# Linear attention and two feed-forward layers on one core: loads one step earlier, stores one slot later, transposed sums in their own slot, and one unbroken run for the first layer's g

## The chip, the cores and the metric

The kernel runs on one core of one Trainium2 chip. The metric is device time in microseconds (us), the median of several executions. Beside it one execution was profiled, and every row below comes from that one.

## What is computed

Attention over 8 batches, 8 heads, 576 positions and head size 64, with a feature map of 128 columns used twice (once with each sign), followed by two feed-forward layers over 4608 tokens of width 512:

```python
def phi(x):
    proj = np.einsum('bhsd,df->bhsf', x, w_phi)
    proj = proj - np.max(np.abs(proj), axis=-1, keepdims=True)
    return np.concatenate([np.exp(proj), np.exp(-proj)], axis=-1)
...
kv = np.einsum('bhsf,bhsd->bhfd', k_p, v);  z = np.sum(k_p, axis=2)
num = np.einsum('bhsf,bhfd->bhsd', q_p, kv)
den = np.einsum('bhsf,bhf->bhs', q_p, z)[..., None] + 1e-06
x = num / den                       # then (tokens, heads * 64)
h = x @ w_in;  g = h - np.tanh(h);  x = g @ w_out          # first layer, 512 -> 2048 -> 512
out = ((x @ w1) * (x @ w2)) @ w3 @ w_out                   # second layer
```

## The kernel before

**Attention.** The program is written out by hand, and each engine runs its instructions in that order. Two batches with one head form a pair, so there are 32 pairs, and 33 steps, since a step holds the keys of one pair and the queries of the pair before it. A step has 9 tiles of 128 positions; four tiles make a slot, and slots do not line up with steps (9 slots cover 4 steps). In a slot `s` PE (TensorE) does, in this order: the projections of the slot's four tiles for q and k (`p_pe`, line 188), the transposes of the q tiles of slot s-1 (`t_pe`, 229), the products of keys and values of slot s-2 (`kv_pe`, 266), half an output of a pair where one is due (`o_pe`, 319 and 328), and, after the slot in which a pair's sums have been completed, two transposes and four small sums (`kv_turn`, 301 and 305). DVE (VectorE) takes maximum and difference of q and of k (`p_max`, 195 and 197), copies the finished sums out of the accumulator (`kvs`, 296), copies them again when they are transposed (`kvx`, 310), and copies every second output half (`st`, 340). PE's output needs `kvx`. ACT (ScalarE) does the exponentials, POOL (GpSimd) sums over keys. Pieces of the first layer's weights are turned from 64-bit floats into a high and a low 32-bit part in the gaps (`conv_steps`): `FC_EARLY` of 16 chunks per weight within the attention, the rest in the first layer.

In the kernel before the sums go through three slots: completed in one, copied (`kv_copy`) and transposed (`kv_turn`) in the next, copied again (`kv_out`) in the third, which is the slot where the output needs them. The SP queue issues all loads and stores: `qk` and `v` of step st+2 behind the last tile of step st, with two buffers for `qk` and three for `v`, and an output's stores right behind its copy.

**First layer.** 9 blocks of 512 tokens by 16 chunks of hidden features give 144 steps. In step n PE does `mm1(n)` (12 matmuls into `h`) and `mm2(n-2)` (12 matmuls of g's high and low part, `gh` and `gl`, into four accumulators `y`). Between the two stands `act_g`: ACT makes `u`, `t`, `s` (lines 480 to 482), DVE does five operations (486, 488, 490, 492, 494), ACT rounds the result to `gh` (498), POOL takes the rest as `gl` (499). Up to six operations of the weight conversions stand between DVE's five (`some()`), the others behind `gl`. At the end of a block the four `y` are copied out, three on ACT and one on DVE (513, 515). The second layer comes behind, and its code is not touched.

Of the kernel before, what the change touches and what calls it, by code (L numbers as in the profile page):

```python
# [45 lines left out]
TINY = 2.0 ** -15  # L46
FC_EARLY = 13


@with_exitstack  # L50
def kernel(ctx, tc, qk_in, v_in, w_phi, w_in, w_out, w12, w3t_in, wo2, out):
# [19 lines left out]
    slots = {}  # L71
    late = []

    def slot(kind, i, shape):
# [9 lines left out]
    def conv_steps(pool, pre, n, load, dst, nb=1):  # L84
# [7 lines left out]
        def s_abs():  # L92
            o["t"] = pool.tile([128, n], U32, tag=f"{pre}t", name=f"{pre}t", bufs=nb)
            ACT.activation(o["t"].bitcast(F32), words(o["raw"], F32)[1], ACTF.Abs)
# [23 lines left out]
        def s_lo():  # L118
            POOL.tensor_tensor(o["lo"], o["t"].bitcast(F32), o["hi"].bitcast(F32), ALU.subtract)

        return [s_load], [s_abs, s_max, s_shift], [s_c, s_a], [s_add], [s_hi], [s_lo]

# [26 lines left out]
    def attention():  # L149
        with ExitStack() as es:  # L150
# [19 lines left out]
            def load_step(st):  # L170
                qk[st] = pool.tile([128, PT], F32, tag="qk", name="qk")
                SP.dma_start(qk[st], qk_in[st])
                if st < NPAIR:
                    vv[st] = pool.tile([128, TPP + 1, D], F32, tag="v", name="v", bufs=3)
                    SP.dma_start(vv[st], v_in[st])
# [160 lines left out]
            def o_out(st, c, ps):  # L336
                bp, h = divmod(st - 1, H)
                t = pool.tile([128, CW + CE], F32, tag="st", name="st")
                if c:
                    DVE.tensor_copy(t, ps[:, :CW + CE])  # L340
                else:
                    ACT.activation(t, ps[:, :CW + CE], ACTF.Copy)
                for b in range(2):
                    c0 = bp * PT + b * S + c * CW
                    SP.dma_start(num_d[h * D:(h + 1) * D, c0:c0 + CW], t[b * D:(b + 1) * D, :CW])
                    for e in range(2):
                        r = 64 * b + 32 * e
                        SP.dma_start(den_d[bp, h:h + 1, c0 - bp * PT + e * CE:c0 - bp * PT + (e + 1) * CE], t[r:r + 1, CW:])
                return bp if c and h == H - 1 else None
# [36 lines left out]
            ok = lambda g: 0 <= g < n_slots  # L386
            kv_done, turned, todo_o = None, None, []
            for s in range(n_end):
# [7 lines left out]
                if ok(s):  # L396
                    p_pe(s)
                if kv_done is not None:
                    kv_copy(kv_done)
                if ok(s - 1):  # L400
# [3 lines left out]
                if ok(s):  # L404
                    dq[s] = p_max(s, pq, q_js(s), "q")
                for st, c, ps in todo_o:
                    bp = o_out(st, c, ps)
                    if bp == NBP - 1:
                        pending.extend([lambda: recip_load(NBP - 1), lambda: recip(NBP - 1)])
                    elif bp is not None:  # L410
                        recip_load(bp)
                        extra[s + 4].append(lambda bp=bp: recip(bp))
                if turned is not None:
                    kv_out(turned)
                some(2)
                turned = kv_done
                if ok(s - 1):
                    q_exp(s - 1, 0)
                    q_exp(s - 1, 1)
                    kv_sum(s - 1)  # L420
                kv_done = kv_pe(s - 2) if ok(s - 2) else None
                if ok(s):
                    dk[s] = p_max(s, pk, k_js(s), "k")
                todo_o = [(st, c, o_pe(st, c)) for st, c in o_at.get(s, [])]
                if turned is not None:
                    kv_turn(turned)
                some(99)
                for n in tiles_of(s) if ok(s) else ():
                    st, t = where(n)
                    if t == TPP - 1 and st + 2 < n_steps:  # L430
                        load_step(st + 2)
# [29 lines left out]
    def moe1():  # L461
        with ExitStack() as es:
# [6 lines left out]

            def act_g(n, x, ys):  # L470
                def some():
                    if x:
                        x.pop(0)()
# [15 lines left out]
                some()  # L489
                DVE.scalar_tensor_tensor(p, s, C0, p, ALU.add, ALU.mult)  # L490
                some()
                DVE.tensor_scalar(u, u, TLIM * TLIM, None, ALU.is_le)  # L492
                some()
                DVE.copy_predicated(t, u.bitcast(U32), p)  # L494
                some()
# [4 lines left out]
                y_out(ys, 3)  # L500
                del hh[n]
                gg[n] = gh, gl
# [15 lines left out]
            def mm2(n):  # L518
# [4 lines left out]
                gh, gl = gg.pop(n)  # L523
                for d in range(NK):
                    c = slice(d * 128, (d + 1) * 128)
                    for m, (w, x) in enumerate(((wh, gh), (wl, gh), (wh, gl))):
                        PE.matmul(  # L527
                            yy[j][d], w[:, c], x, start=i == 0 and m == 0, stop=i == NFC - 1 and m == 2
                        )
                return (j, yy.pop(j)) if i == NFC - 1 else None  # L530
# [49 lines left out]
            for n in range(n_all + LAG):  # L580
# [17 lines left out]
                if n < n_all:  # L598
                    x = list(extra.get(n, []))
                    act_g(n, x, ys)  # L600
                    for f in x:
                        f()
                    if i % 3 == 0 and i < 12:
# [201 lines left out]
```

## Time and profile before

| | |
|---|---|
| median of 3 runs | 1864.66 us (1863.5 to 1865.66) |
| profiled execution | 1864.26 us, of which the profile's span is 1862.5 us |
| PE, matmuls | busy 1797.4 us, 97% of the span |
| DVE, ACT, POOL | busy 53%, 42%, 40% |
| DMA | 168.86 MB, 91 GB/s over the span |

A share is an average over the whole span; attention, first and second layer differ much. A busy PE is not a PE at full rate: a matmul's recorded time overlaps that of the next one, so the distance from one start to the next tells the rate.

### The profile page before, as it was taken

How to read it: one execution, taken by the hardware profiler on the slowest of the kernel's cores; microseconds unless marked ns; L12 is line 12 of the kernel's file. 1: busy time of each engine (PE TensorE's matmuls, PEld its weight loads, DVE VectorE, ACT ScalarE, POOL GpSimd, SP SyncE). 2: the span in 40 equal slices, each digit the busy share in tenths (PEclk: the TensorE clock that was granted, in tenths of full speed). 3: DMA queues.
4: the chain of work that ended last, by engine and by line, in shares of the span. 5: the costliest groups of instructions: out<-in, count | busy, mean ns of one | idle time of the engine just before them, and what ended most of it. 6: DMA issues, size and time to landing. Idle time of an engine off the chain costs nothing.

```text
span 1862.5 us, 27570 instructions
## 1 busy us (share of the span) xinstructions
PE 1797.4 (97%) x10176; PEld 1409.6 (76%) x10176; DVE 995.1 (53%) x1649; ACT 785.0 (42%) x1601; POOL 744.3 (40%) x750
## 2 busy tenths in 40 slices
PE   7999899999999999999999999999999999999999
PEld 5666666667777777777777777878888888888887
DVE  6777777847677777777777776521121112112111
ACT  4656566535555555545555555422122112112211
POOL 5767677725455655555555564300011001001100
PEclk9999999999999999999999999999999999999999
DMA  4444445422233333333333324552001101100100
GB/s 151 143 144 153 148 152 175 122 65 64 65 94 96 99 101 108 100 97 100 99 98 102 114 91 148 174 175 84 30 23 40 34 29 29 41 34 23 35 23 23
DMA packets 99944, 168.86 MB, mean 91 GB/s; under 512 B 13920, under 2 KB 46048, under 8 KB 99808
## 3 DMA queue, kind: packets, MB, share of 16 engines
q1 hardware_dynamic: 99648, 167.02, 28.6%
q8 instruction: 80, 1.31, 0.3%
q14 instruction: 56, 0.46, 0.1%
q10 hardware_dynamic: 160, 0.07, 0.0%
HBM read 117.46 MB, written 49.58 MB: 90 GB/s over the span
## 4 chain that ended last, share of the span: by engine, by line
PE 52%; DVE 22%; ACT 16%; issue 5%; DMA 3%; SPq 1%; ACTq 0%; DVEq 0%; POOL 0%
PE ab L456 21%; PE o L657 11%; DVE p L490 6%; DVE t L494 6%; ACT gh L498 4%; DVE u L492 4%; PE y L527 3%; ACT u L480 3%; PE p L188 3%; PE h L456 3%; ACT s L482 3%; PE o L319 3%; PE o L680 2%; PE kv L266 2%; DVE et L104 2%
## 5 line engine op out<-in xcount | busy, mean ns | idle before, releaser
L499 POOL TENSOR_TENSOR gl<-t,gh 128x512 fp32r<-128x512 f32 x144 | 186.6, 1296 | 287.6 <-ACT gh L498 202.9
L748 POOL TENSOR_TENSOR xl<-xn,xh 128x512 fp32r<-128x512 f32 x72 | 93.6, 1299 | 498.7 <-ACT xh L747 498.6
L498 ACT ACTIVATE gh<-t 128x512 fp32r<-128x512 f32 x144 | 91.0, 632 | 367.0 <-DVE t L494 338.9
L527 PE MATMUL y<-gl,woh 128*128 128x512 f32 x576 | 231.4, 402 | 13.9 <-POOL gl L499 12.8
L527 PE MATMUL y<-gh,woh 128*128 128x512 f32 x576 | 228.2, 396 | 14.6 <-DVE yo L515 7.1
L486 DVE SCALAR_TENSOR_TENSOR p<-h,u 128x512 f32<-128x512 f32 x144 | 99.6, 692 | 234.5 <-ACT t L481 234.5
L527 PE MATMUL y<-gh,wol 128*128 128x512 f32 x576 | 224.8, 390 | 0.0
L456 PE MATMUL h<-xh,wih 128*128 128x512 f32 x576 | 224.3, 389 | 0.0
L456 PE MATMUL h<-xh,wil 128*128 128x512 f32 x576 | 224.1, 389 | 0.0
L456 PE MATMUL h<-xl,wih 128*128 128x512 f32 x576 | 224.1, 389 | 0.0
L456 PE MATMUL ab<-xh,wih 128*128 128x512 f32 x576 | 224.1, 389 | 0.0
L456 PE MATMUL ab<-xh,wil 128*128 128x512 f32 x576 | 224.1, 389 | 0.0
L456 PE MATMUL ab<-xl,wih 128*128 128x512 f32 x576 | 224.1, 389 | 0.0
L639 DVE TENSOR_TENSOR t<-ab,a 128x512 f32<-128x512 f32 x72 | 49.8, 692 | 297.4 <-PE ab L456 294.4
L527 PEld LDWEIGHTS y<-gl,woh 128*128 128x128 f32 x576 | 108.0, 188 | 60.1 <-POOL gl L499 38.6
L527 PEld LDWEIGHTS y<-gh,woh 128*128 128x128 f32 x576 | 108.2, 188 | 45.1 <-DVE yo L515 10.1
L195 DVE TENSOR_REDUCE m<-p 128x4 f32<-128x512 f32 (+1 forms) x145 | 98.7, 681 | 80.4 <-PE p L188 80.0
L494 DVE COPY_PREDICATED t<-u,p 128x512 f32<-128x512 uint32 x144 | 127.4, 885 | 3.2
L208 ACT ACTIVATE kp<-dk 128x512 f32<-128x512 f32 x144 | 82.9, 626 | 109.6 <-DVE dk L197 75.3
L490 DVE SCALAR_TENSOR_TENSOR p<-s,p 128x512 f32<-128x512 f32 x144 | 128.2, 890 | 0.0
L456 PEld LDWEIGHTS h<-xh,wih 128*128 128x128 f32 x576 | 108.1, 188 | 22.8 <-issue 0.2
L456 PEld LDWEIGHTS h<-xh,wil 128*128 128x128 f32 x576 | 108.2, 188 | 22.6
(106 smaller groups left out, 3539.7 us busy)
## 6 DMA issues: line engine op xcount, KB each, us to landing
qk<-in_qk SPq DMA_DIRECT2D x33, 576.0 KB
v<-in_v SPq DMA_DIRECT2D x32, 320.0 KB
xn<-y_d SPq DMA_DIRECT2D x37, 256.0 KB
num_d<-st SPq DMA_DIRECT2D x128, 72.0 KB
xn<-num_d SPq DMA_DIRECT2D x36, 256.0 KB
out<-o SPq DMA_DIRECT2D x36, 256.0 KB
y_d<-yo SPq DMA_DIRECT2D x35, 256.0 KB
eraw<-in_w SPq DMA_DIRECT2D x32, 256.0 KB
```

Of the source, the lines that this page charges most:

```text
L195: DVE.tensor_reduce(m[:, :n], what[g][:, j], AX.X, ALU.max, apply_absolute_value=True)
L208: ACT.activation(kp[g][:, sgn, span(js)], dk[g][:, span(js)], ACTF.Exp, scale=1.0 - 2 * sgn)
L456: PE.matmul(ps, a[:, kk, :], b[kk], start=m == 0, stop=m == 3 * NK - 1)
L486: DVE.scalar_tensor_tensor(p, h, C2, u, ALU.mult, ALU.mult)
L490: DVE.scalar_tensor_tensor(p, s, C0, p, ALU.add, ALU.mult)
L492: DVE.tensor_scalar(u, u, TLIM * TLIM, None, ALU.is_le)
L494: DVE.copy_predicated(t, u.bitcast(U32), p)
L498: ACT.activation(gh, t, ACTF.Copy)
L499: POOL.tensor_tensor(gl, t, gh.bitcast(F32), ALU.subtract)
L527: PE.matmul(yy[j][d], w[:, c], x, start=i == 0 and m == 0, stop=i == NFC - 1 and m == 2)
L657: PE.matmul(ps, a[:, c], w, start=m == 0, stop=m == 23)
L748: POOL.tensor_tensor(lo, a, hi.bitcast(F32), ALU.subtract)
```

## The change

`qk` gets three buffers and `v` four, and both are loaded behind the first tile of step st, not the last. The output's stores are listed in the next slot, and the four small stores of the denominators become one. A pair's sums are copied and transposed in the slot that completes them, and copied again at the start of the next slot. `FC_EARLY` falls from 13 to 12 (the buffers take its room), so the first layer converts 16 half chunks and not 12; their stages are split in one more step and 14 steps hold their starts. In the first layer DVE's five operations stand together; ACT's conversions stand before `gh`, DVE's and POOL's behind `gl`. The copy of the fourth `y` moves up to DVE's third place. In `mm2`, except for the first and last chunk of a block, the four matmuls on `gl` come last. The buffers of the converted word `et` go from 3 to 4; the raw words `eraw` keep 2.

```diff
-FC_EARLY = 13
+FC_EARLY = 12
...
-                qk[st] = pool.tile([128, PT], F32, tag="qk", name="qk")
+                qk[st] = pool.tile([128, PT], F32, tag="qk", name="qk", bufs=3)
...
-                    vv[st] = pool.tile([128, TPP + 1, D], F32, tag="v", name="v", bufs=3)
+                    vv[st] = pool.tile([128, TPP + 1, D], F32, tag="v", name="v", bufs=4)
...
                 if ok(s):
                     p_pe(s)
+                for x_ in todo_store:
+                    bp = o_store(*x_)
...
                 if kv_done is not None:
-                    kv_copy(kv_done)
+                    kv_out(kv_done)
+                todo_store = [o_out(*x_) for x_ in todo_o]
...
-                if turned is not None:
-                    kv_out(turned)
-                some(2)
-                turned = kv_done
...
                 kv_done = kv_pe(s - 2) if ok(s - 2) else None
+                some(2)
+                if kv_done is not None:
+                    kv_copy(kv_done)
                 if ok(s):
                     dk[s] = p_max(s, pk, k_js(s), "k")
                 todo_o = [(st, c, o_pe(st, c)) for st, c in o_at.get(s, [])]
-                if turned is not None:
-                    kv_turn(turned)
+                if kv_done is not None:
+                    kv_turn(kv_done)
                 some(99)
...
-                    if t == TPP - 1 and st + 2 < n_steps:
+                    if t == 0 and st + 2 < n_steps:
                         load_step(st + 2)
...
                 DVE.scalar_tensor_tensor(p, h, C2, u, ALU.mult, ALU.mult)
-                some()
                 DVE.tensor_tensor(t, h, t, ALU.subtract)
-                some()
+                y_out(ys, 3)
                 DVE.scalar_tensor_tensor(p, s, C0, p, ALU.add, ALU.mult)
...
+                for f in x:
+                    if f in on_act:
+                        f()
                 gh = p3.tile([128, 512], F32R, tag="gh", name="gh")
...
+                todo = [(d, m) for d in range(NK) for m in range(3)]
+                if 0 < i < NFC - 1:
+
+                    todo.sort(key=lambda a: a[1] == 2)
...
-            for i in range(FC_EARLY, NFC):
-                for f in (w_in_chunk, w_out_chunk):
+            for f in (w_in_chunk, w_out_chunk):
+                for i in range(FC_EARLY, NFC):
                     for part in range(2):
                         c = f(p2, i, part, 2, "e", 3)
-                        late_chunks.append([c[0], c[1], c[2] + c[3] + c[4] + c[5]])
+                        late_chunks.append([c[0], c[1], c[2] + c[3], c[4] + c[5]])

             for i, c in enumerate(late_chunks):
-                place(c, i)
+                place(c, i * 14 // len(late_chunks))
```

DVE early in the attention, from one slot's maximum of q to the next slot's. `m` and `dq`, `dk` are maxima and differences, `ct` a weight conversion, `st` an output half. Before:

```order
L195 TENSOR_REDUCE m<-p 128x4
L197 TENSOR_TENSOR dq<-p,m 128x512
L340 COPY st<-o 128x432
L310 COPY kvx<-kv 128x260
L104 SCALAR_TENSOR_TENSOR ct<-craw,ct 128x512
L195 TENSOR_REDUCE m<-p 128x4
L197 TENSOR_TENSOR dk<-p,m 128x512
L296 COPY kvs<-kv 128x256
L195 TENSOR_REDUCE m<-p 128x4
```

And now, in the same slot:

```order
L342 COPY st<-o 128x432
L197 TENSOR_REDUCE m<-p 128x4
L199 TENSOR_TENSOR dq<-p,m 128x512
L105 SCALAR_TENSOR_TENSOR ct<-craw,ct 128x512
L298 COPY kvs<-kv 128x256
L197 TENSOR_REDUCE m<-p 128x4
L199 TENSOR_TENSOR dk<-p,m 128x512
L312 COPY kvx<-kv 128x260
L197 TENSOR_REDUCE m<-p 128x4
```

`kvs` has moved ahead of the slot's k, and `kvx` to the head of the next slot, ahead of its q; the copy `st` has moved to the head of its slot.

DVE in the first layer, step 30, from the first of g's operations to the last conversion (`et` is a piece of the second layer's weights). Before:

```order
L486 SCALAR_TENSOR_TENSOR p<-h,u 128x512
L488 TENSOR_TENSOR t<-h,t 128x512
L104 SCALAR_TENSOR_TENSOR et<-eraw,et 128x256
L490 SCALAR_TENSOR_TENSOR p<-s,p 128x512
L492 TENSOR_SCALAR u<-u 128x512
L494 COPY_PREDICATED t<-u,p 128x512
L98 TENSOR_SCALAR et<-et 128x256
L101 TENSOR_SCALAR et<-et 128x256
```

And now:

```order
L489 SCALAR_TENSOR_TENSOR p<-h,u 128x512
L490 TENSOR_TENSOR t<-h,t 128x512
L492 SCALAR_TENSOR_TENSOR p<-s,p 128x512
L493 TENSOR_SCALAR u<-u 128x512
L494 COPY_PREDICATED t<-u,p 128x512
L105 SCALAR_TENSOR_TENSOR et<-eraw,et 128x256
L99 TENSOR_SCALAR et<-et 128x256
L102 TENSOR_SCALAR et<-et 128x256
```

All conversions of the step now stand behind g's five operations.

ACT in step 2 of the first layer, where half chunks are converted (`et<-eraw` takes up a raw piece for the first time, `ec<-eraw` reads an older one again). Before:

```order
L480 ACTIVATE u<-h 128x512
L481 ACTIVATE t<-h 128x512
L482 ACTIVATE s<-u,c_sb 128x512
L109 ACTIVATE ec<-eraw 128x256
L116 ACTIVATE wih_5238<-et 128x256
L94 ACTIVATE et<-eraw 128x256
L498 ACTIVATE gh<-t 128x512
```

And now:

```order
L484 ACTIVATE u<-h 128x512
L485 ACTIVATE t<-h 128x512
L486 ACTIVATE s<-u,c_sb 128x512
L110 ACTIVATE ec<-eraw 128x256 x2
L95 ACTIVATE et<-eraw 128x256
L502 ACTIVATE gh<-t 128x512
```

Two pieces are under way instead of one. The third piece, which `et<-eraw` takes up here, is loaded into a raw buffer that the first piece frees with its last DVE operation (line 105 of the changed kernel), and that operation now stands behind g's five of this same step.

## Rows read from the trace of the kernel before

**Rows 1.** Busy time by stretch: attention, first layer, second layer (us, instruction counts)

```profile
41.10:389.00 347.90, 326.63 (x3689) 223.25 (x3689) 259.88 (x430) 203.16 (x442) 242.77 (x288) 1.00 0.46 142
389.00:1231.50 842.50, 814.04 (x3484) 645.98 (x3480) 591.17 (x1007) 441.68 (x915) 436.40 (x396) 1.00 0.33 103
1231.50:1862.00 630.50, 626.20 (x2760) 518.03 (x2760) 118.36 (x171) 120.83 (x202) 41.46 (x32) 1.00 0.13 42
```

**Rows 2.** Timeline, two slots: start, duration, engine, line [idle before, releaser]

```profile
321.04 1.08 PE L266 MATMUL kv<-kp,v 128*64 128x256 f32 x8
...
322.40 0.42 DVE L310 COPY kvx<-kv 128x260 f32<-128x260 f32 x1
...
322.87 1.19 PE L319 MATMUL o<-qp,kvx 128*64 128x288 f32 x8 [0.75 <-DVE kvx L310]
...
326.29 1.08 PE L266 MATMUL kv<-kp,v 128*64 128x256 f32 x8
...
327.21 1.14 PE L319 MATMUL o<-qp,kvx 128*64 128x288 f32 x8
```

**Rows 3.** Waits within 41 to 389 us: sum, times, longest

```profile
PE o L319 <- DVE kvx L310: 9.6, 17, 1.3
...
PE kv L266 <- DVE kvx L310: 6.4, 6, 2.2
...
PE p L188 <- DMA qk<-in_qk: 2.7, 3, 1.4
```

**Rows 4.** Timeline, a projection whose load was late

```profile
158.03 0.72 PE L188 MATMUL p<-wphi,qk 64*128 64x128 f32 x8 [1.15 <-DMA qk<-in_qk]
```

**Rows 5.** Stretches at the start, columns as in rows 1, PE's clock third last

```profile
25.00:27.00 2.00, 0.42 (x6) 0.36 (x4) 1.97 (x4) 2.00 (x6) 2.00 (x4) 1.00 0.06 25
27.00:35.00 8.00, 8.00 (x49) 5.58 (x47) 6.35 (x11) 3.90 (x8) 6.59 (x8) 0.57 0.32 97
```

**Rows 6.** Timeline of the first layer's first step, conversions and POOL absent

```profile
395.32 0.69 DVE L486 SCALAR_TENSOR_TENSOR p<-h,u 128x512 f32<-128x512 f32 x1 [5.59 <-ACT t L481]
...
397.58 0.72 DVE L494 COPY_PREDICATED t<-u,p 128x512 f32<-128x512 uint32 x1
...
398.34 0.63 ACT L498 ACTIVATE gh<-t 128x512 fp32r<-128x512 f32 x1 [2.51 <-DVE t L494]
...
399.98 0.69 DVE L486 SCALAR_TENSOR_TENSOR p<-h,u 128x512 f32<-128x512 f32 x1 [1.67 <-ACT t L481]
```

**Rows 7.** Groups of the first layer, 389 to 1231 us: count, busy, mean ns

```profile
L499 POOL TENSOR_TENSOR gl<-t,gh 128x512 fp32r<-128x512 f32 x144 | 186.6, 1296 | 287.6 <-ACT gh L498 202.9 <-issue 49.0 <-DMA xr<-rden_d 24.3
L490 DVE SCALAR_TENSOR_TENSOR p<-s,p 128x512 f32<-128x512 f32 x144 | 128.2, 890 | 0.0
L494 DVE COPY_PREDICATED t<-u,p 128x512 f32<-128x512 uint32 x144 | 127.4, 885 | 3.2
...
L492 DVE TENSOR_SCALAR u<-u 128x512 f32<-128x512 f32 x144 | 87.2, 605 | 0.0
...
L104 DVE SCALAR_TENSOR_TENSOR et<-eraw,et 128x256 uint32<-128x256 uint32 x92 | 47.6, 517 | 0.0
...
L747 ACT ACTIVATE xh<-xn 128x512 fp32r<-128x512 f32 x36 | 22.2, 616 | 0.0
```

**Rows 8.** Waits of the first layer, 389 to 1231 us

```profile
DVE p L486 <- ACT t L481: 234.5, 144, 5.6
...
PE y L527 <- POOL gl L499: 12.8, 25, 0.7
...
PE y L527 <- DVE yo L515: 7.1, 7, 1.3
...
ACT u L480 <- PE h L456: 4.2, 8, 0.6
```

**Rows 9.** A raw piece's load and the DMA after it (last two columns: share, GB/s)

```profile
407.38 0.34 SPq L145 DMA_DIRECT2D eraw<-in_w_out  x1
...
410.00:411.00 1.00, 1.00 (x6) 0.65 (x4) 0.75 (x3) 0.61 (x2) 0.00 (x0) 1.00 0.00 0
```

More of the change, by code (lines that the diff above doesn't have):

```diff
@@ L72 @@
     late = []
+    on_act = set()
     def slot(kind, i, shape):
@@ L92, in s_abs @@
         def s_abs():
-            o["t"] = pool.tile([128, n], U32, tag=f"{pre}t", name=f"{pre}t", bufs=nb)
+            o["t"] = pool.tile([128, n], U32, tag=f"{pre}t", name=f"{pre}t", bufs=nb + (nb > 1))
             ACT.activation(o["t"].bitcast(F32), words(o["raw"], F32)[1], ACTF.Abs)
@@ L119, in s_lo @@
             POOL.tensor_tensor(o["lo"], o["t"].bitcast(F32), o["hi"].bitcast(F32), ALU.subtract)
+        on_act.update((s_abs, s_c, s_hi))
         return [s_load], [s_abs, s_max, s_shift], [s_c, s_a], [s_add], [s_hi], [s_lo]
@@ L337, in o_out @@
                 bp, h = divmod(st - 1, H)
-                t = pool.tile([128, CW + CE], F32, tag="st", name="st")
+                t = pool.tile([128, CW + CE], F32, tag="st", name="st", bufs=3)
                 if c:
@@ L342, in o_out, with o_store @@
                     ACT.activation(t, ps[:, :CW + CE], ACTF.Copy)
+                return t, bp, h, c
+            def o_store(t, bp, h, c):
                 for b in range(2):
@@ L345, in o_out @@
                     SP.dma_start(num_d[h * D:(h + 1) * D, c0:c0 + CW], t[b * D:(b + 1) * D, :CW])
-                    for e in range(2):
-                        r = 64 * b + 32 * e
-                        SP.dma_start(den_d[bp, h:h + 1, c0 - bp * PT + e * CE:c0 - bp * PT + (e + 1) * CE], t[r:r + 1, CW:])
+                d = den_d[bp, h, c * CW:]
+                SP.dma_start(
+                    bass.AP(tensor=d.tensor, offset=d.offset, ap=[[S, 2], [CE, 2], [1, CE]]),
+                    t.rearrange("(a p) n -> a p n", p=32)[:, 0, CW:],
+                )
                 return bp if c and h == H - 1 else None
@@ L386, in attention @@
             ok = lambda g: 0 <= g < n_slots
-            kv_done, turned, todo_o = None, None, []
+            kv_done, todo_o, todo_store = None, [], []
             for s in range(n_end):
@@ L397, in attention @@
                     p_pe(s)
+                for x_ in todo_store:
+                    bp = o_store(*x_)
+                    if bp == NBP - 1:
+                        pending.extend([lambda: recip_load(NBP - 1), lambda: recip(NBP - 1)])
+                    elif bp is not None:
+                        recip_load(bp)
+                        extra[s + 4].append(lambda bp=bp: recip(bp))
                 if kv_done is not None:
-                    kv_copy(kv_done)
+                    kv_out(kv_done)
+                todo_store = [o_out(*x_) for x_ in todo_o]
                 if ok(s - 1):
@@ L405, in attention @@
                     dq[s] = p_max(s, pq, q_js(s), "q")
[L406 to L412, printed above, removed]
-                if turned is not None:
-                    kv_out(turned)
-                some(2)
-                turned = kv_done
                 if ok(s - 1):
@@ L468, in moe1, with act_g @@
             gg, yy = {}, {}
[L470 to L473, printed above, removed]
+            def act_g(n, ys):
                 h = hh[n]
@@ L484, in act_g @@
                     y_out(ys, d)
-                some()
                 DVE.scalar_tensor_tensor(p, h, C2, u, ALU.mult, ALU.mult)
-                some()
                 DVE.tensor_tensor(t, h, t, ALU.subtract)
-                some()
+                y_out(ys, 3)
                 DVE.scalar_tensor_tensor(p, s, C0, p, ALU.add, ALU.mult)
-                some()
                 DVE.tensor_scalar(u, u, TLIM * TLIM, None, ALU.is_le)
-                some()
                 DVE.copy_predicated(t, u.bitcast(U32), p)
-                some()
+                x = extra.get(n, [])
+                for f in x:
+                    if f in on_act:
+                        f()
                 gh = p3.tile([128, 512], F32R, tag="gh", name="gh")
@@ L499, in act_g @@
                 POOL.tensor_tensor(gl, t, gh.bitcast(F32), ALU.subtract)
-                y_out(ys, 3)
                 del hh[n]
@@ L523, in mm2 @@
                 gh, gl = gg.pop(n)
[L524 to L529, printed above, removed]
+                todo = [(d, m) for d in range(NK) for m in range(3)]
+                if 0 < i < NFC - 1:
+                    todo.sort(key=lambda a: a[1] == 2)
+                for d, m in todo:
+                    w, x = ((wh, gh), (wl, gh), (wh, gl))[m]
+                    PE.matmul(
+                        yy[j][d], w[:, d * 128:(d + 1) * 128], x,
+                        start=i == 0 and m == 0, stop=i == NFC - 1 and m == 2,
+                    )
                 return (j, yy.pop(j)) if i == NFC - 1 else None
@@ L598, in moe1 @@
                 if n < n_all:
[L599 to L602, printed above, removed]
+                    act_g(n, ys)
+                    for f in extra.get(n, []):
+                        if f not in on_act:
+                            f()
                     if i % 3 == 0 and i < 12:
```

## The prediction

> **What bounds the kernel now.** I read the busy time by stretch first, because the shares over the whole span hide which engine waits. In the second layer PE has 2760 matmuls in 626.2 busy us, one every 0.2269 us, without a pause worth naming. The first layer has the same kind of matmul, 144 steps of 24 and 24 more from the second layer's first two halves, 3480 in all; at that rate they need 789.6 us, and the stretch lasts 842.5 us. So 52.9 us are lost there, though PE reads busy in 814 of 842.5 us [rows 1]. In the attention PE is the busiest too (326.6 of 347.9 us), DVE next with 259.9 (75%).
>
> Then the timeline, for what a lost moment looks like. In a slot without a wait the output starts 0.92 us behind the key-value products (326.29 to 327.21); in the slot before it 1.83 us, waiting for `kvx`, which ended at 322.82 [rows 2]. The recorded wait is 0.75, the loss 0.91: a stop costs 0.16 us beyond its recorded length.
>
> Then the table of waits. In the attention PE waits for `kvx` 9.6 and 6.4 us, 23 times, and 2.7 us, 3 times, for `qk` [rows 3]. In the first layer it waits for `gl` (25 times) and for the copies of `y` [rows 8]; and behind that, DVE's first operation of every step waits for ACT's `t`, 234.5 us in 144 steps, while ACT's `u` almost never waits for PE's `h` (8 times, 4.2 us). The pace of that layer is thus set by a loop of DVE and ACT: five operations, `gh`, `u`, `t`, and round again; PE stands behind it. All matmuls are at the full clock but for a short stretch at the start [rows 1, 5].
>
> **The change part by part.** The sum is made against the profiled execution's 1864.26 us, which is 0.4 us under the median; a difference of 0.2% (3.7 us) is about what a measurement of this kernel can tell from none.
>
> *Sums a slot earlier (gain 19.7).* `kvx` now runs at the head of the slot after the one that completes the sums, and the output needs it one slot later still. The 23 waits go: 16.0 us recorded and 23 times 0.16 beyond, 19.7 us [rows 2, 3]. The new wait is PE's transposes for `kvs` in the same slot; between them and the key-value products stands an output half, at least 1.19 us of PE work, and the copy takes DVE some 0.42 (as `kvx`) [rows 2], so it is covered unless DVE is over 0.8 us late. Behind `kvs` on DVE stands the slot's k, for which the next slot's projections wait. In the first few slots no output half is due, and there I count neither gain nor loss.
>
> *Loads a step earlier (gain 3.2).* The wait of 1.15 us at 158.03 and two like it go [rows 3, 4]: 2.7 us and three times 0.16. The merged stores take issues off SP; SP has no other wait on PE's path, so this counts nothing, as does the later listing of the stores, for which a third `st` buffer is there.
>
> *What DVE takes back (loss 5).* Without PE's pauses DVE has 259.9 us of work in some 325 us, 80%, but not evenly: every nine slots two short ones follow each other (one with no sums to transpose, then one without an output), and DVE has as much to do in them as in others: two maxima, two differences, a copy, often a conversion. The trace has no row for this; bounds are 0 (DVE catches up, as it does in most such places now) and 10 (over 1 us in each of 8 rounds, as much as the wait it replaces). I take 5. Attention: 19.7 + 3.2 - 5 = 18.
>
> *First layer, the loop.* In the first step, with POOL idle, the five operations take from 395.32 to 398.30, and from there to the next first operation it is 1.68 us: a loop of 4.66 us [rows 6]. In the mean over all steps the last three are longer by 0.21, 0.19 and 0.165 (890, 605 and 885 ns against 0.68, 0.42 and 0.72 in that step), in all 0.57. Every fourth step on average ACT also splits an `x` in between, 36 times 0.616 us, 0.15 a step [rows 7]. So the bare loop is 5.38 us, PE's step 24 times 0.2269, 5.45. What made the loop longer are DVE's conversions between the five; behind them they fall into the 1.68 us in which DVE waits for ACT anyway (the largest, `et`, takes 0.52 [rows 7]; all three of a piece, by that row an estimate of 1.2, and 0.64 pieces a step). If that cover were gone they would cost up to 0.8 us a step. The loop falls just under PE's step, and PE becomes the bound. With `gl` last in 14 of 16 chunks POOL has 6 matmuls, 1.36 us, more time; and the fourth `y` is copied before DVE's third operation, so the waits for `y` go too. Of the 52.9 us I keep: 0.7 for the first `gl`, which is still wanted third; an estimated 6 for the unevenness of a loop that is only 1% under PE's step (bounds 0 and 13, a quarter of today's loss); and the next item.
>
> *Late half chunks (loss 6).* In steps 2, 8 and 9 ACT takes up a raw piece whose buffer is freed only in the same step, by the conversion behind g's five operations, and `gh` stands behind it. From the end of the five it is 0.52 for `et`, then the load: issued at 407.38, its data were in before 410.00, so at most 2.6 us [rows 7, 9]; with ACT's 0.4 some 3.5 us in which `gh`, the next `u` and all behind them stand. `gh` is otherwise 2.8 us ahead (12 matmuls three times are 8.2 us, the way from `h` to `gh` about 5.4). One such step alone costs 3.5 less some 1.8 of lead at the start, two in a row 7.0 less 2.8: together 6. Bounds: 0, if the copy of the load comes sooner than it shows, and 10 without any lead. The lower `FC_EARLY` moves two chunks' work from one layer to the other and counts nothing beyond this.
>
> First layer: 52.9 - 0.7 - 6 - 6 = 40. **Sum:** 1864.3 - 18 - 40 = 1806.
>
> **Where a rule would have it otherwise.** The last three of g's operations [rows 6, 7] are 0.57 us a step above the undisturbed ones, no more, though POOL works in about half of that time. The Trainium skill, "SBUF — State Buffer", section "Who interferes with whom", says that VectorE and GpSimd share a pair of ports under an exclusive lock, and whichever comes second stands still until the first is done. By this rule a run of DVE's three operations beside `gl` could lose a whole `gl` in each step; by the trace it does so in part.
>
> **The rivals.**
> 1. *The loop stays the bound.* If the gathered run meets POOL more often and loses 0.8 instead of 0.57, the loop is 5.61; 144 of them and 13 us of start and tail are 821, with 6 for the late chunks 827: the layer gains 15 only. 1864.3 - 18 - 15 = 1831. For it: only 1% between the loop and PE's step. Against it: POOL's conversions now come after `gl`, so more of them fall on DVE's conversions and on the 1.68 us without work, not on the last three operations.
> 2. *The attention's gain is spent elsewhere.* PE stops for `dq` where it stopped for `kvx`, and only 5 of 22.9 us stay: 1819. For it: DVE at 80%. Against it: 80% still leaves DVE 65 us, and `dq` is made ahead of what the slot adds.
> 3. *Slower.* The gathered run waits out a whole `gl` (1.30 us) in every step: loop 6.1, layer 13 + 880 + 6 = 899, 57 more than now: 1903. From 1.03 us a step on (loop 5.84, layer 860) the attention's 18 are eaten up and the kernel is slower. Against it: the mean of 0.57, which already holds many meetings.
> 4. *All of it.* DVE takes nothing back, only 2 us stay in the first layer, and the half clock near 28 us, which followed a stretch with PE busy 0.42 of 2 us [rows 5], does not come (8 us at a mean of 0.57 cost 3.4): 1864.3 - 22.9 - 50.9 - 3.4 = 1787.
>
> **Chances.** Forecast 0.58, with a range of its own from 1797 to 1817; rival 1 0.14, rival 2 0.13, rival 3 0.05, rival 4 0.06, and 0.04 for what I have not seen. From 1789 to 1833 lie the forecast, rivals 1 and 2. Faster by over 0.2%: 0.94; within 0.2%: 0.02; slower: 0.04, since rival 3 mostly ends beyond its deciding point.
>
> **What would show it.** Attention: no wait of the output for `kvx`; from key-value products to output 0.92 us in each slot; waits of projections for `dq` show what was given back. First layer: a block of 16 steps in 87 to 88 us where it is some 92.5 now (842.5 less the ends, over nine), DVE's wait for `t` much shorter, `u` now waiting for `h` often, and three waits of ACT for `eraw` near the layer's beginning, each with a stop of PE. The prediction is wrong if `u` still hardly ever waits for `h`: then the loop is still the bound.

## The result and the profile after

The changed kernel takes 1875.73 us (median of 4 runs, 1873.54 to 1877.36) beside 1864.91 for the kernel before: ratio 1.0058, 95% interval 1.0041 to 1.0076. It is 0.6% slower, where 1806 was forecast. The profiled execution is 1876.69 us, its span 1874.9.

Busy time by stretch of the changed kernel, columns as in [rows 1]: attention, first layer, second layer, then two places around a stop of PE (one in the attention, one in the first layer):

```profile
41.10:404.60 363.50, 338.40 (x3712) 234.09 (x3708) 255.52 (x427) 203.09 (x441) 237.61 (x285) 0.96 0.43 131
404.60:1244.50 839.90, 810.56 (x3484) 654.78 (x3480) 583.79 (x1019) 456.37 (x927) 415.01 (x404) 0.99 0.33 104
1244.50:1874.90 630.40, 625.91 (x2761) 517.94 (x2760) 118.35 (x171) 120.84 (x202) 41.46 (x32) 1.00 0.13 42
...
95.00:98.60 3.60, 1.03 (x20) 0.40 (x16) 3.56 (x8) 3.09 (x6) 2.23 (x3) 1.00 0.18 42
98.60:100.70 2.10, 1.98 (x24) 1.97 (x26) 1.78 (x4) 0.67 (x2) 1.54 (x2) 0.99 0.93 240
100.70:104.10 3.40, 3.40 (x21) 2.09 (x20) 2.67 (x4) 2.08 (x4) 2.78 (x4) 0.50 0.47 170
...
881.00:885.70 4.70, 2.83 (x13) 1.78 (x11) 1.40 (x4) 2.00 (x5) 1.08 (x2) 1.00 0.80 284
885.70:889.10 3.40, 3.40 (x8) 2.73 (x9) 2.10 (x6) 1.69 (x4) 0.98 (x1) 0.51 0.59 198
```

The attention is 15.6 us longer, the first layer only 2.6 shorter, the second the same. PE's clock, 1.00 in the attention before, is 0.96: stretches at the lower level have appeared, each behind a stop of PE. The waits of the attention, 41.1 to 404.6 us, which answer to [rows 3], with one line of the kernel before (41 to 389 us) behind them:

```profile
DVE ct L99 <- ACT ct L95: 41.9, 22, 4.1
...
ACT qp L252 <- PE o L330: 36.2, 15, 3.2
...
PE kv L303 <- DVE kvs L298: 22.9, 16, 3.0
...
DVE ct L98 <- ACT ct L94: 7.0, 7, 2.0
```

The waits for `kvx` and `qk` are gone, as forecast. In their place PE stops for `kvs`, 22.9 us in 16 places; DVE, which makes `kvs`, itself waits 41.9 us for ACT's first conversion operation `ct` (7.0 us in 7 places in the kernel before, the last line). The timeline shows the chain once, and the end of a block in the first layer (durations can overlap the next row's start):

```profile
91.82 0.89 ACT L252 ACTIVATE qp<-tr 128x128 f32<-128x128 f32 x4 [2.15 <-PE o L330]
92.57 0.69 ACT L95 ACTIVATE ct<-craw 128x512 f32<-128x512 f32 x1
...
93.30 0.43 DVE L99 TENSOR_SCALAR ct<-ct 128x512 f32<-128x512 f32 x1 [3.36 <-ACT ct L95]
...
97.14 1.20 DVE L105 SCALAR_TENSOR_TENSOR ct<-craw,ct 128x512 uint32<-128x512 uint32 x1
...
98.26 0.41 DVE L298 COPY kvs<-kv 128x256 f32<-128x256 f32 x1
...
98.72 0.44 PE L303 MATMUL kv<-ident,kvs 128*128 128x128 f32 x2 [2.69 <-DVE kvs L298]
...
101.19 1.11 PE L231 MATMUL tr<-ident,dq 128*128 128x128 f32 x4
...
880.79 1.58 ACT L516 ACTIVATE yo<-y 128x512 f32<-128x512 f32 x3
...
882.28 3.67 SPq L519 DMA_DIRECT2D y_d<-yo  x4
...
884.91 0.69 DVE L518 COPY yo<-y 128x512 f32<-128x512 f32 x1 [3.30 <-DMA y_d<-yo]
...
885.66 0.75 PE L533 MATMUL y<-gh,woh 128*128 128x512 f32 x1 [1.87 <-DVE yo L518]
```

ACT's `ct` now stands behind the exponentials `qp` (here behind their wait of 2.15 us for PE's output), DVE stands 3.36 us for it, everything behind it on DVE is late, `kvs` too, and PE stops 2.69 us. From 100.7 on PE's clock is at 0.50, the 1.2 GHz level, and four transposes take 1.11 us (0.66 at the full clock). The last rows are the first layer's matter: the fourth copy of `y` waits 3.30 us for the store of the first, whose buffer it takes, now with three of g's operations behind it. The first layer's waits, 404.6 to 1244.5 us, the wait of the fourth copy in the kernel before, and the three last of g's operations in the changed kernel:

```profile
DVE yo L518 <- DMA y_d<-yo: 21.9, 7, 4.6
...
PE y L533 <- ACT gh L502: 14.9, 17, 3.4
...
PE y L533 <- DVE yo L518: 9.9, 6, 2.9
...
ACT et L95 <- DMA eraw<-in_w_out: 9.7, 2, 5.0
...
ACT et L95 <- DMA eraw<-in_w_in: 5.4, 1, 5.4
...
ACT u L484 <- PE h L464: 3.4, 6, 0.6
...
PE y L533 <- POOL gl L503: 0.7, 1, 0.7
```

```profile
DVE yo L515 <- DMA y_d<-yo: 0.6, 2, 0.3
```

```profile
L492 DVE SCALAR_TENSOR_TENSOR p<-s,p 128x512 f32<-128x512 f32 x144 | 148.4, 1030 | 0.0
L494 DVE COPY_PREDICATED t<-u,p 128x512 f32<-128x512 uint32 x144 | 110.0, 764 | 4.9
...
L493 DVE TENSOR_SCALAR u<-u 128x512 f32<-128x512 f32 x144 | 80.3, 558 | 0.0
```

`gl` holds PE up for 0.7 us now (12.8 before), but the fourth copy, `gh` and three loads of `eraw` do so instead. In the order of the program (492, 493, 494) the three operations are 0.35, 0.14 and 0.04 us above those of the undisturbed step of [rows 6], together 0.53, where I had 0.57.

### The profile page after: what moved, and what is told of

Same layout as the page of the kernel before. It is cut to its first block, busy times and chain, and to the rows that moved or that the text cites. A ratio compares the mean times of both kernels' runs of the same rounds, so it can differ in the third digit from the quotient of the medians.

```text
span 1874.9 us, 27168 instructions
## 1 busy us (share of the span) xinstructions
PE 1804.7 (96%) x10176; PEld 1428.9 (76%) x10176; DVE 980.3 (52%) x1655; ACT 798.1 (43%) x1607; POOL 716.8 (38%) x754
## 4 chain that ended last, share of the span: by engine, by line
PE 65%; DVE 17%; ACT 10%; issue 4%; DMA 3%; POOL 1%; SPq 1%; ACTq 0%; DVEq 0%; POOLq 0%
PE ab L464 21%; PE o L664 10%; PE y L533 10%; PE h L464 9%; DVE p L492 4%; DVE t L494 3%; PE p L190 3%; DVE p L489 3%; PE kv L268 3%; ACT gh L502 3%; PE o L687 2%; PE o L321 2%; DVE u L493 2%; ACT u L484 2%; ACT t L485 2%
## 5 line engine op out<-in xcount | busy, mean ns | idle before, releaser
L533 PE MATMUL y<-gh,woh 128*128 128x512 f32 x576 | 232.1, 403 | 24.8 <-ACT gh L502 14.9
L533 PE MATMUL y<-gl,woh 128*128 128x512 f32 x576 | 164.3, 392 | 0.7 <-POOL gl L503 0.7
L492 DVE SCALAR_TENSOR_TENSOR p<-s,p 128x512 f32<-128x512 f32 x144 | 148.4, 1030 | 0.0
L533 PEld LDWEIGHTS y<-gh,wol 128*128 128x128 f32 x576 | 109.7, 190 | 26.4 <-POOL wol L120 5.0
L464 PEld LDWEIGHTS h<-xl,wih 128*128 128x128 f32 x576 | 108.8, 189 | 22.9
L464 PEld LDWEIGHTS ab<-xh,wih 128*128 128x128 f32 x576 | 108.1, 188 | 22.5
```

Of the source, the lines that this page charges most:

```text
L464: PE.matmul(ps, a[:, kk, :], b[kk], start=m == 0, stop=m == 3 * NK - 1)
L533: PE.matmul(yy[j][d], w[:, d * 128:(d + 1) * 128], x, start=i == 0 and m == 0, stop=i == NFC - 1 and m == 2,)
```

## The experiments

Theory A: in the attention the only harmful edit is that `some(2)` (the conversions) moved behind `q_exp`, on ACT above all. Theory B: in the first layer PE is the bound nearly everywhere, and single places (the fourth copy, the late half chunks) eat the gain. Rivals: the sums' own slot leaves `kvs` no room whatever stands ahead (against A); the loop of DVE and ACT is still the bound (against B). Attention's end and the layer's length below are those of the profiled execution.

**One half of the change each.** The first kernel has the changed attention and the first layer's old order of operations (the late half chunks stay as changed), the second the old attention and the changed first layer.

```diff
# first, against the changed kernel
-            def act_g(n, ys):
+            def act_g(n, x, ys):
...
-                    todo.sort(key=lambda a: a[1] == 2)
# second, against the kernel before
-            o["t"] = pool.tile([128, n], U32, tag=f"{pre}t", name=f"{pre}t", bufs=nb)
+            o["t"] = pool.tile([128, n], U32, tag=f"{pre}t", name=f"{pre}t", bufs=nb + (nb > 1))
...
+                y_out(ys, 3)
...
+                    todo.sort(key=lambda a: a[1] == 2)
```

> The changed attention (with 12 chunks converted early and the rest late, as in the changed kernel), but the first layer's operations of g, the copies of y and the order of the second products as before. In the changed kernel the attention ends 15.6 us later than before (404.6 against 389.0) and the first layer is 2.6 us shorter (839.9 against 842.5). If the loss is the attention's own, this run is at 1876 to 1888 us. If the two parts disturb each other (a later start of loads, stores at the border), it is at 1866 or below.

Measured: 1882.93 us, ratio 1.0107 (1.0092 to 1.0122). Attention to 399.7 us; PE waits 23.1 us for `kvs`, DVE 41.8 for `ct`, as in the changed kernel.

> The attention as before, with 13 chunks converted early; the first layer as changed. Theory 1, the new waits of the first layer are its own (DVE's fourth copy of y waiting for a store, 21.9 us over 7 borders, and a loop that stays at 5.7 us): 1855 to 1862 us, a few us less than before, since only the late chunks' waits for loads go. Rival: the layer suffers from the half clock and the late chunks alone; then it shows what was forecast for it, 1825 to 1840 us.

Measured: 1848.43 us, ratio 0.9922 (0.9907 to 0.9937). The first layer takes 827.0 us, 15.5 less than before, with 12 late half chunks and 1.0 us of waits for `eraw` in all; the fourth copy still waits 24.2 us for stores. Neither of the two ranges held. So the loss is the attention's, and the layer's part gains, but less than 40.

**The conversions ahead of the exponentials, all else as changed.** On ACT the conversions move ahead of the queries' exponentials, on POOL ahead of the sums over keys; the orders of DVE and PE stay as they are.

```diff
+                some(2)
                 if ok(s - 1):
                     q_exp(s - 1, 0)
...
                 kv_done = kv_pe(s - 2) if ok(s - 2) else None
-                some(2)
```

> The changed kernel with the two conversion operations listed ahead of the queries' exponentials again; on DVE nothing moves, on ACT the first conversion stands ahead of the exponentials. Theory 1: DVE waits 41.9 us for that conversion, which stands behind exponentials that wait for PE; the sums' copy stands behind it, PE's transposes stop for the copy 22.9 us, and after such stops the clock is at half. Then DVE's wait falls below 10 us, PE's stops for the copy below 8, and the time to 1835 to 1850 us. Theory 2: copying and transposing in the slot that completes the sums is too tight by itself; then PE's stops stay above 15 us and the time above 1865.

Measured: 1835.73 us, ratio 0.9854 (0.9838 to 0.9871). The attention ends at 363.7 us instead of 404.6. Its waits, and the stretches of attention and first layer:

```profile
DVE ct L99 <- ACT ct L95: 3.3, 5, 2.0
...
PE kv L303 <- DVE kvs L298: 1.0, 1, 1.0
```

```profile
41.10:363.70 322.60, 320.58 (x3661) 222.78 (x3656) 254.28 (x420) 199.54 (x433) 238.59 (x284) 0.99 0.48 145
363.70:1204.20 840.50, 811.98 (x3484) 656.49 (x3480) 583.29 (x1019) 455.98 (x927) 414.39 (x404) 0.99 0.33 104
```

One moved line is worth 40 us: the waits for `ct` and `kvs` go together, and the clock is back at 0.99. Of the 40.9 us in the attention 21.9 are waits of PE for `kvs`; the lower clock is an estimate of 11 more (0.04 of 363.5 us less 0.01 of 322.6). Theory A is shown; that it is ACT's order and not POOL's rests on the waits, which name ACT's `ct`, and not on a run that moves one without the other. The first layer has hardly changed (840.5 against 839.9).

**The copy of the sums ahead of the conversions on DVE, ACT's order as changed.**

```diff
-                some(2)
                 if kv_done is not None:
                     kv_copy(kv_done)
+                some(2)
```

> The changed kernel with the sums' copy ahead of the two conversion operations on DVE; ACT as in the changed kernel. Theory 1 (the copy is late because it stands behind a conversion that waits for ACT): PE's stops for the copy go below 8 us, the half clock in the attention with them, the time to 1835 to 1855 us, though DVE still waits for the conversion ahead of the keys' maximum, so some stops of the projections come instead. Theory 2 (too tight by itself): stops stay above 15 us, time above 1865.

Measured: 1860.57 us (1853.67 to 1869.53, 10 runs), ratio 0.9992 (0.9973 to 1.001). DVE still waits 37.6 us for `ct`, and PE 12.4 us for `kvs` in 10 places. This lies between the two theories: 15 of the 40 us come back. The copy is ahead of its own slot's conversions, but DVE stands for `ct` nearly as long as before, and what is behind that is still late. The rest of the cure is the place of the conversions ahead of the exponentials.

**A buffer of its own for the fourth copy of `y`**, from here on with the conversions ahead. It takes one of `u`'s two, which is free there.

```diff
+                elif d == 3:
+                    t = p2.tile([128, 512], F32, tag="u", name="u")
```

> The changed kernel with the weight conversions ahead of the exponentials (the run of 1835.73 us), and besides the fourth copy of y takes a buffer of u's pair instead of the first copy's, so DVE no longer waits there for a store. In the run of 1835.73 that wait was 21.6 us in 7 places, and PE's step behind it took 7.13 us in the mean instead of 5.44, the next one 6.00. Theory: PE is the bound in nearly every other step (5.44 us) and this wait is the largest single loss left; it goes and takes 8 times 1.7 us with it, and perhaps some of the stretches at half clock behind those stops: 1815 to 1823. Rival one: the loop of DVE and ACT sets the pace everywhere, so DVE only waits for t instead: 1831 to 1837. Rival two: PE must wait for that copy in any case, since it stands behind two of g's operations (the kernel before lost 2.1 us at this place with hardly any wait for a store): 1829 to 1835, with the step still near 7.

Measured: 1812.8 us, ratio 0.9728 (0.9712 to 0.9743): 20 us of the first layer (820.4) for one wait. The profiled execution, 1817.42 us, is the slowest of the four. The step behind the copy takes 5.72 us instead of 7.13, and no half clock follows. The rival "the loop is the bound everywhere" falls.

**Loads late again and 13 chunks early.**

```diff
-FC_EARLY = 12
+FC_EARLY = 13
...
-                    if t == 0 and st + 2 < n_steps:
+                    if t == TPP - 1 and st + 2 < n_steps:
```

> The kernel of the run with the free fourth copy, and besides q, k and v loaded behind the last tile of a step with 2 and 3 buffers as before the change, and 13 chunks converted within the attention (12 late half chunks instead of 16). Theory: the earlier loads are worth about 3 us (three waits for qk come back, 2.7 us), while four more late half chunks cost about 13 (three steps near the layer's start took 11.5, 7.3 and 10.8 us instead of 5.44): 8 to 12 us less than that run. Rival: the attention needs the loads now that it is faster, and the waits for qk come back larger: no gain or a loss.

Measured: 1818.09 us, ratio 0.9755 (0.9729 to 0.978). Both sides moved: the first layer gains 19.4 us, to 801.0, and the attention loses 19.2, ending at 384.1. In the first layer, 384.1 to 1185.1, and then the attention:

```profile
ACT gh L502 <- PE y L535: 12.2, 11, 1.9
...
PE y L535 <- ACT gh L502: 4.2, 9, 0.7
...
ACT u L484 <- PE h L464: 3.1, 6, 0.6
```

```profile
PE p L190 <- DMA qk<-in_qk: 7.0, 3, 2.5
...
PE kv L303 <- DVE kvs L298: 4.7, 3, 2.1
```

The 801.0 us are what I had forecast for the layer (802), with PE waiting 4.2 us for `gh`; and still `u` hardly waits for `h`. When the loop is ahead, it is `gh` that waits for `y`, for a free buffer of its pair, so my sign for "PE is the bound" looked at the wrong instruction.

**The old order of `mm2`'s products, on the kernel just told.**

```diff
-                if 0 < i < NFC - 1:
-                    todo.sort(key=lambda a: a[1] == 2)
```

> The kernel of the run before this one (loads late, 13 early), with the products of mm2 in the order of before the change in every chunk (high, low, high by gl for each of four quarters). By the prediction's count PE's waits for gl come back: 25 of 12.8 us in the kernel before, with what a stop costs besides up to 17 us more. Rival: POOL's conversions now stand behind gl, which is early enough even as the third matmul: 0 to 4 us more.

Measured: 1819.15 us, ratio 0.9754 (0.9739 to 0.9769): no difference. PE's waits for `gl` do come back in part, 5.5 us in 12 places for 0.7 in one, but those for `gh` fall from 4.2 to 0.2. Where POOL's conversions stand behind `gl`, its place in `mm2` no longer matters to the time.

**The conversions between g's operations again, on that same kernel.**

```diff
                 DVE.scalar_tensor_tensor(p, h, C2, u, ALU.mult, ALU.mult)
+                some()
                 DVE.tensor_tensor(t, h, t, ALU.subtract)
+                some()
...
```

> The kernel of the run with loads late and 13 early, with the conversions of the first layer again between DVE's five operations of g, in the order of before the change; all else stays. If the loop of DVE and ACT is what paces the layer, about 0.64 pieces a step of some 1.2 us of DVE lengthen it from 5.4 to about 5.8 to 6.0 us: 144 steps, 40 us more at most, and 20 at least. If PE has a lead that hides it, or if what the run gives back elsewhere is as much: 0 to 8 us more.

Measured: 1862.95 us, ratio 0.9989 (0.9978 to 1.0). The first layer is 843.6 us instead of 801.0. The unbroken run is worth 43 us, a little above the range given. The edit takes ACT's and POOL's conversions back among g's operations too, so the 43 us are the price of all three places; PE now waits for `gh` 16.4 us in 27 places and for `gl` 4.7 in 9. The mean distance between starts of `mm1` (my count in the traces; 24 matmuls at 0.2269 are 5.45), steps 3 to 17 in sum and later ones by their place in the block; place 3, the step behind that of the copies, is left out of the last column (5.70 in the changed kernel, 5.44 to 5.46 in the other five):

| kernel | steps 3-17 | place 2 | 8 / 11 / 14 | others, without 3 |
|---|---|---|---|---|
| before | 92.1 | 7.53 | 5.64 / 6.02 / 6.00 | 5.59 |
| changed | 102.4 | 7.22 | 5.88 / 5.73 / 5.93 | 5.47 |
| fourth copy free | 102.7 | 5.72 | 5.52 / 5.66 / 5.85 | 5.45 |
| loads late, 13 early | 83.5 | 5.60 | 5.60 / 5.63 / 5.92 | 5.45 |
| conversions between | 90.3 | 6.53 | 6.01 / 6.06 / 6.04 | 5.69 |
| pairs of half chunks | 94.4 | 5.50 | 5.60 / 5.64 / 5.86 | 5.45 |

With the run unbroken PE is the bound, at 5.45 to 5.47, in the changed kernel too. With the conversions between, the loop is the bound in part of the steps: of the 94 outside places 2, 8, 11 and 14, 42 take over 5.5 us there and 29 in the kernel before, 12 in the changed kernel and one or two where the fourth copy is free. Theory B holds, with its places: the end of a block (place 2), and the first 15 steps, which want 81.7. Places 8, 11 and 14 stay 0.1 to 0.5 us above 5.45 where the fourth copy is free too, an estimate of 6 us in the layer; no run was made on them.

**The late half chunks in pairs**, on the kernel with the fourth copy free (loads early, 12 chunks).

```diff
+                        if f is w_out_chunk and i == NFC - 1:
+                            late_chunks.append([c[0], c[1], c[2] + c[3] + c[4] + c[5]])
...
-                place(c, i * 14 // len(late_chunks))
+                place(c, i // 2 * 2)
```

> The kernel of the run with the free fourth copy (1812.8 us; loads early, 12 chunks converted in the attention), with the 16 late half chunks started in pairs every second step, 0 to 14, and the last pair in three steps instead of four; so no raw piece waits for a buffer that its own step frees. Theory: what is left in the first layer are the waits of ACT for eraw near its start; steps of 11.6, 7.6 and 10.8 us there come down to about 6, and with the half clock behind them 13 to 18 us go: 1795 to 1800. Rival: two pieces at once lengthen DVE's and ACT's steps, and the same time is lost in smaller parts (steps of 6.4 us, as in the kernel with 12 halves): 1806 to 1813.

Measured: 1807.61 us (1805.57 to 1808.32), ratio 0.9692 (0.9675 to 0.9708), the fastest of all. Attention, first and second layer:

```profile
41.10:362.20 321.10, 319.07 (x3661) 221.94 (x3657) 254.15 (x420) 199.62 (x433) 239.45 (x284) 1.00 0.48 146
362.20:1173.30 811.10, 798.05 (x3484) 651.92 (x3480) 581.37 (x1019) 456.05 (x927) 415.09 (x404) 1.00 0.34 108
1173.30:1803.80 630.50, 626.09 (x2760) 517.86 (x2760) 118.33 (x171) 120.84 (x202) 41.46 (x32) 1.00 0.13 42
```

The layer gains 9.3 us, less than the theory had, and the time is in the rival's range. Steps 3 to 17 are still 12.7 us above 81.7: about half of it lies in steps 8 to 15, which take 5.4 to 7.0 us (the rival had 6.4), and half in step 16, where the last pair is ready late, with one stop of PE:

```profile
459.28 0.79 PE L535 MATMUL y<-gh,wol 128*128 128x512 f32 x1 [4.24 <-POOL wol L120]
```

**The attention's other parts, one undone at a time.** Loads late (on the kernel with the fourth copy free); the sums in three slots (on the one with pairs); and on top of that the copies `st` behind q's difference.

```diff
# loads late
-                    if t == 0 and st + 2 < n_steps:
+                    if t == TPP - 1 and st + 2 < n_steps:
...
# three slots
-                    kv_out(kv_done)
+                    kv_copy(kv_done)
...
+                if turned is not None:
+                    kv_out(turned)
+                turned = kv_done
# copies of the outputs back
-                todo_store = [o_out(*x_) for x_ in todo_o]
                 if ok(s - 1):
                     k_exp(s - 1, 0)
...
+                todo_store = [o_out(*x_) for x_ in todo_o]
                 if turned is not None:
                     kv_out(turned)
```

> The kernel of the run with the free fourth copy (1812.8 us), with q, k and v loaded behind the last tile of a step, two buffers for q and k, three for v, as before the change; 12 chunks stay. In the run with these loads and 13 chunks the attention ended at 384.1 us, against 364.9. Theory one: the loads are what it needs, since PE no longer wastes time elsewhere (7.0 us of waits for qk in 3, and stops and half clock behind them): the attention ends at 378 to 384, 1826 to 1832 in all. Theory two, by the prediction's count: 3.2 us only, and the thirteenth chunk's conversions cost the rest: it ends near 368 to 370, 1816 to 1818.

Measured: 1821.67 us, ratio 0.9766 (0.9751 to 0.978). The attention ends at 370.5, 5.6 us later, near theory two, but the time is 8.9 us longer, between the two ranges. The two profiled executions differ at their start, where PE's mean clock up to 41.1 us is 0.96 here and 0.88 in the kernel with the fourth copy free, so 5.6 is rather too little. Beside the run with loads late and 13 chunks this one shows the thirteenth chunk alone: without it the attention ends 13.6 us earlier (370.5 for 384.1) and the first layer takes 18.0 longer (819.0 for 801.0).

> The kernel of the run with pairs of half chunks, with the sums again going through three slots (copied out and transposed in the slot behind the one that completes them, copied again in the third). By the prediction's term the 23 waits for kvx come back, 16.0 us and 23 times 0.16 beyond: 19 to 20 us more than that run. Rival one: stops bring stretches at half clock with them, and it is 25 us or more. Rival two: with loads early and the conversions ahead, DVE is early enough for the copies and PE hardly waits: 0 to 8 us more.

Measured: 1814.85 us, ratio 0.9728 (0.9714 to 0.9743), 7.2 us above the kernel with pairs; the attention ends at 371.7, 9.5 us later. Its waits for `kvx`:

```profile
PE o L321 <- DVE kvx L312: 2.2, 9, 0.4
PE kv L268 <- DVE kvx L312: 1.0, 3, 0.3
```

The 23 waits did not come back: rival two.

> The kernel with the sums in three slots (1814.85 us, attention to 371.7), with the copies of the output halves (st) moved from the head of the slot back behind q's difference, ahead of kvx, where they stood before the change. In the kernel before PE waited for kvx 16.0 us in 23 places; in the kernel with three slots it is 3.2 us in 12. Theory: the place of st made that difference, since DVE copies st just ahead of kvx; the waits come back, 13 us and what a stop costs besides, and the attention ends at 382 to 390: 1825 to 1833. Rival: earlier loads and merged stores made it; then nothing returns: 1813 to 1817.

Measured: 1826.11 us, ratio 0.9802 (0.9785 to 0.9818); the attention ends at 382.8, another 11.1 us later, and here most of them are again, 11.4 us in 20 places:

```profile
PE o L321 <- DVE kvx L312: 8.9, 17, 0.8
...
PE kv L268 <- DVE kvx L312: 2.5, 3, 0.8
```

So two edits cure [rows 3]: undone one behind the other, the sums' own slot is worth 9.5 and the earlier place of `st` 11.1 us of the attention, by the medians of the runs 7.2 and 11.3. `st` was moved back only with the sums in three slots; whether the sums' own slot would do without it was not tried. With the loads (5.6) the parts come to 26.2 us, and the fastest kernel gains 26.8 in the attention (347.9 to 321.1), but that they meet is luck: the thirteenth chunk (13.6, with loads late) is not among them, so the parts depend on each other and do not simply add up.

## Why the prediction was wrong

The forecast was too low by 70 us: some 34 in the attention (18 shorter forecast, 15.6 longer measured) and some 37 in the first layer (40 shorter forecast, 2.6 measured).

- **The step that failed** is "*Sums a slot earlier*", in its sentence that the copy `kvs` "is covered unless DVE is over 0.8 us late". DVE is so late that PE waits up to 3.0 us for it, since the change also puts the conversions behind `q_exp` on ACT. The moved line stands in the diff and its operation in the rows of DVE's order, yet the prediction prices it nowhere and never names ACT's queue in the attention. It cost 40.9 us of the attention (404.6 against 363.7), more than all that the other edits bring there.
- The gain itself was sized nearly right: 19.7 forecast, 9.5 and 11.1 measured with both edits undone, but the place of `st`, which I had not counted, has a part in it, and how large a part by itself stays open. Loads: 3.2 forecast, 5.6 measured by the attention's end and 8.9 by the medians. The fall of `FC_EARLY` I had put at nothing beyond the late half chunks: with the loads late it shortens the attention by 13.6 us and lengthens the first layer by 18.0. "What DVE takes back", 5 forecast: no more than the 1.4 us of waits for `kvs` and `dq` that the fastest kernel still has.
- *First layer, the loop*: that the unbroken run puts the loop just under PE's step held (5.45 to 5.47 in the other steps, 43 us for the run). But "The pace of that layer is thus set by a loop" was true of part of the kernel before only: 65 of the 94 steps outside places 2, 8, 11 and 14 took no more than 5.5 us there too. And my sign, `u` waiting for `h`, fails as told above: by it (3.4 us in 6 places) the loop would still be the bound. "So the waits for `y` go too" failed: the copy was moved ahead on DVE, to where the store of the first copy has not landed, and 21.9 us of waits for the store (0.6 before) came into the loop itself; with a free buffer the layer is 20 us shorter.
- *Late half chunks* were forecast at 6 us of loss. Steps 3 to 17 of the changed kernel take 102.4 us where 81.7 would do and the kernel with 13 early chunks takes 83.5: a loss of some 19. I had priced the three waits for `eraw` (in one of them `gh` starts 3.3 us behind the end of g's operations, where I had 3.5) and not what they push back: a last weight that comes too late for PE, and the lower clock behind each stop. How the 13 us beyond the forecast are shared between these was not tried.
- Of the rivals, none was the case. The third had the right sign for a wrong reason. The second, "the attention's gain is spent elsewhere", named `dq` as the new wait and stopped at zero; a new wait can cost more than the one that it replaces.
- All was mended by three small edits; the kernel that has them takes 1807.61 us, but that does not make the forecast of 1806 right for the kernel that was asked about.

## What to carry to other kernels

When a line of a hand-written order moves, list what it issues on every engine, and read on each queue what it is now behind: an operation that DVE waits for, put behind one of ACT's that waits for PE, closes a loop through three engines. A copy moved ahead needs its buffer earlier as well; look up when the store that frees it lands. And to tell whether the fastest engine is the bound, compare the distance of its steps with its own work, since the instruction that waits when the loop is ahead may be one that wants a buffer.

## What the runs showed of the hardware

A stop of PE cost more than its length. In the changed kernel 12 stretches at 0.5 of the clock lie behind the start, each behind a stop of PE of 1.85 to 3.44 us; one stop of 2.33 us, at 1068.5, had none, and neither had one of 2.19 us in the kernel before. The length alone does not decide it: with the conversions ahead a stretch at 0.5 from 249.7 lies behind a stop of only 1.03 us. The mean clock over the span is 0.985 in the changed kernel and 0.998 before, which is an estimate of at most some 24 us of full clock less over 1875 us. The Trainium skill, "TensorE: Matmul & The Clock Gate", section "Part 1: The HAM clock gate (the "warmup" mystery)", says that the low level is the resting state and that work lifts it; the trace agrees, with 0.50 behind the stop at 96.0 and 1.00 from 104.1 on. Which stop brings the lower level and which does not was not tried, and stays open; that the stops bring it at all is read from the traces, where stops and low stretches went together (the attention has 0.96 with 22.9 us of stops for `kvs`, 0.99 with 1.0), not from an experiment on the clock alone.

The first of the last three of g's operations on DVE (`p<-s,p`) is 1.03 us in the mean against 0.68 in the undisturbed first step. The Trainium skill, "SBUF — State Buffer", section "Who interferes with whom", has one of the two engines stand still until the other is done; the mean of 0.53 us over all three says that far less than a whole `gl` (1.30 us [rows 7]) was lost in a step, and the unbroken run was worth its 43 us all the same.
